# The output tail of an attention and spectral-mixing kernel: other items, and work moved to GpSimd and ScalarE

## The chip, the cores and the metric

The kernel runs on one core of one Trainium2 chip, with the other cores idle. The metric is the device time of one execution in microseconds. The engines are TensorE (PE in the profile, PEld for its weight loads), VectorE (DVE), ScalarE (ACT), GpSimd (POOL) and SyncE (SP), which here only issues DMAs.

## The reference

Attention with two kinds of masks for 8 batches of 576 rows, then a spectral layer. What the tail computes stands in the last lines:

```python
X = np.fft.rfft(x, axis=1)
Y = np.zeros_like(X)
Xr, Xi = (np.real(X[:, :n_modes]), np.imag(X[:, :n_modes]))
Yr = np.einsum('bmd,mde->bme', Xr, w_r) - np.einsum('bmd,mde->bme', Xi, w_i)
Yi = np.einsum('bmd,mde->bme', Xr, w_i) + np.einsum('bmd,mde->bme', Xi, w_r)
Y[:, :n_modes] = Yr + 1j * Yi
y = np.fft.irfft(Y, n=S, axis=1)
u = x + y
return (u + np.maximum(u @ w_ch, 0.0)).astype(np.float32)
```

Here x is the attention's output (8 batches, S = 576 rows, 512 columns), there are 64 modes, and w_r and w_i are 64 matrices of 512 x 512 each. The output is f32: 8 x 576 x 512 x 4 bytes = 9.44 MB.

## The kernel before

The kernel has three stretches. Attention runs first, with its two mask patterns one after the other. Beside its second half and after it the mode matrices stream in from HBM (cast to f16 on the way, issued from GpSimd's queue) and are multiplied with the spectra. The tail then turns spectra back into rows and writes the output.

The order of the instructions on each engine is the order of the program; no scheduler moves anything. Each engine takes its own instructions in order, and waits only where data or a buffer is missing. Pools hand out buffers in rotation: whoever asks for the next one waits until the last reader of what lay in it is done.

The tail splits the output into 18 items of two halves (128 rows x 512 columns each); 16 of them are four row groups t of two neighbouring batches, one half for each batch, and the last two hold the remaining 64 rows of four batches each. A row group with t = 0 or 1 holds the even or the odd rows of the first 256, t = 2 and 3 those of the next 256. By the time that the tail starts, the modes 0 to 47 are already in two kept parts, v0s (x and y times w_ch, f16) and xos (x plus y, f16); missing are the last 16 modes, whose spectra lie in zzs (times w_ch) and yys, four batches in one tile of 128 rows, 32 rows to a batch.

For item k there are two PSUM accumulators of two banks each:

- V: `v_early(k)` copies v0s in by two matmuls with the identity (line 1010), `new_rows(k, ..., zzs)` adds the last modes by two matmuls of 32 rows (line 1031). `v_done(k)` takes the relu on ScalarE into a buffer rl (line 1054).
- U: `u_early(k)` copies xos in the same way (line 1020), `new_rows(k, ..., yys)` adds the last modes. `u_done(k)` adds U and rl on VectorE into a slot of osb (line 1068), and SyncE stores the slot (line 1071).

In `pooled` halves (three of them before) the identity matmul for x is left out of U; GpSimd adds x to the relu instead (line 1057), ahead of VectorE's add.

The loop goes over steps k: V of item k and U of item k - 1 are made in one step. Items 0 and 1 are finished ahead of the loop, and in step 7 the spectra zzs of batches 4 to 7 are made (`spec_z(3, 1, held)`, line 758, and a ScalarE copy by `act_copy`, line 255). PSUM has three double buffers "p" and one "u": V and every even U take "p", the odd U takes "u". The buffers rl come from two tags with two buffers each,

```python
rl = ptr.tile([128, 2, 576], FP, tag=("xT", "rl")[k // 2 % 2], bufs=2, name="rl")
```

so item k + 4 takes the buffer of item k. osb has ten slots.

Four matmuls of 32 rows run side by side when their rows lie in four different quarters of the 128 partitions (quarter b % 4 for batch b). A3 holds the inverse transform's matrix four times, once for each quarter.

Of the kernel before, what the change touches and what calls it, by code (L numbers as in the profile page):

```python
# [12 lines left out]
AluOp = mybir.AluOpType  # L13
# [3 lines left out]
S = 576  # L17
D = 64
DM = 512
# [37 lines left out]
def kernel(  # L57
# [10 lines left out]
    nc = tc.nc  # L68
# [9 lines left out]
    def psum_pools(**bufs):  # L78
        pctx.close()
        pss.clear()  # L80
        for n, c in bufs.items():
            pss[n] = pctx.enter_context(
                tc.tile_pool(name="ps_" + n, bufs=c, space=PSUM)
            )

    def psum(kind, half=False, pair=False):
        if pair:
            return pss[kind].tile([128, 2, 512], FP, tag=kind, name=kind)
        if half:
            return pss[kind].tile([128, 1024], F16, tag=kind, name=kind)  # L90
        return pss[kind].tile([128, 512], FP, tag=kind, name=kind)
# [150 lines left out]
    def normalise(val, den, n, pieces, dst):  # L242
        rec = pin.tile([128, 8], FP, tag="rec", bufs=4, name="rec")
        nc.vector.reciprocal(out=rec[0:n, 0:pieces], in_=den)  # L244
        nc.vector.tensor_tensor(  # L245
            out=dst,
            in0=val.rearrange("p h (q c) -> p h c q", c=4),
            in1=rec[0:n, 0:pieces]
            .to_broadcast((n, pieces, 64))
            .rearrange("p h (q c) -> p h c q", c=4),  # L250
            op=AluOp.mult,
        )

    def act_copy(out, in_):
        nc.scalar.activation(out=out, in_=in_, func=ACTF.Copy)  # L255
# [463 lines left out]
    def row_cols(b, t):  # L719
        if t < 4:  # L720
            return ds(288 * (t % 2) + 32 * (b % 2) + 128 * (t // 2), 128)
        return ds(S + 64 * (b % 2), 64)
# [32 lines left out]
    def spec_z(g, bq, zp):  # L755
        for e in range(4):
            lhs = YS["YT"][:, e, g, ds(8 * bq, 8), :].rearrange("p x m -> p (x m)")
            nc.tensor.matmul(
                zp, lhs, w_chs["n"][:, e, :], start=(e == 0), stop=(e == 3)
            )  # L760
# [35 lines left out]
    def str_front(b):  # L796
        return [
            lambda: str_v(b, 0), lambda: str_v(b, 1),
            lambda: str_v(b, 2), lambda: str_q(b, 0),
            lambda: str_back(b, 0),  # L800
            lambda: str_back(b, 1), lambda: str_q(b, 1),
            lambda: str_k(b, 0),
            lambda: str_k(b, 1), lambda: str_k(b, 2),
        ]
# [12 lines left out]
    first = str_front(0)  # L817
# [73 lines left out]
    zzs = [ptr.tile([128, DM], F16, name=f"zz{i}") for i in range(B)]  # L891
    yys = [ptr.tile([128, DM], F16, name=f"yy{i}") for i in range(B)]
# [22 lines left out]
    for b in range(B + 1):  # L915
        for t in range(5):
            if b > 0 and (t < 4 or b % 2 == 0):
                work.append(lambda b=b, t=t: premix(b - 1, t))
            if b < B and t < 4:
                half, cp = ((1, 0), (1, 1), (0, 0), (0, 1))[t]  # L920
# [3 lines left out]
    A3 = cs["cFl"].rearrange("p a t m -> p (a t m)")[:, 0 : S + 128]  # L924
# [65 lines left out]
    for n, i in enumerate([3, 5, 7] + list(range(8, 21))):  # L990
        b, t = n // 2, n % 2 * 2
# [1 line left out]
        if n % 4 == 3:  # L993
            late.setdefault(i + (b == B - 1), []).append(lambda b=b: renew(b, (4,)))

    items = []
    for P0 in (0, 2):
        items += [((2 * P, 2 * P + 1), t) for t in range(4) for P in (P0, P0 + 1)]
    items += [(range(b, b + 4), 4) for b in (0, 4)]
    LAST = len(items) - 1  # L1000
    vps, ups, rls, osbs = {}, {}, {}, []

    def own(item, kept, half):
        bs, t = item
        return [kept[b][:, t] for b in bs] if t < 4 else [half[b // 2] for b in bs[::2]]

    def v_early(k):
        vps[k] = psum("p", pair=True)
        for j, r in enumerate(own(items[k], v0s, v0h)):
            nc.tensor.matmul(vps[k][:, j], idn, r, start=True, stop=False)  # L1010

    def pooled(k, j):
        return j == 1 and k in (4, 5, 6)

    def u_early(k):
        ups[k] = psum(("p", "u")[k % 2], pair=True)
        for j, r in enumerate(own(items[k], xos, xoh)):
            if pooled(k, j):
                continue
            nc.tensor.matmul(ups[k][:, j], idn, r, start=True, stop=False)  # L1020

    def new_rows(k, acc, spectra):
        bs, t = items[k]
        for j, b in enumerate(bs):
            q = ds(32 * (b % 4), 32)
            i = j // 2 if t == 4 else j
            o, cols = acc[:, i], row_cols(b, t)
            if t == 4:
                o = acc[ds(64 * (b % 2), 64), i]
            fresh = spectra is yys and pooled(k, i)  # L1030
            nc.tensor.matmul(  # L1031
                o, A3[q, cols], spectra[b // 4][q], start=fresh, stop=True
            )

    def out_rows(b, t):
        if t < 4:
            steps = [[2 * DM, 128], [(S + 64) * DM, 2], [1, DM]]
            first = 256 * (t // 2) + t % 2
        else:
            steps = [[DM, 128], [2 * S * DM, 2], [1, DM]]  # L1040
            first = 512
        return bass.AP(
            tensor=out.tensor, offset=out.offset + (S * b + first) * DM, ap=steps
        )

    def pieces(k):
        return [slice(0, 1), slice(1, 2)] if k in (0, 4, 5, 6) else [slice(0, 2)]

    def v_done(k):
        rl = ptr.tile([128, 2, 576], FP, tag=("xT", "rl")[k // 2 % 2], bufs=2, name="rl")  # L1050
        rls[k] = rl[:, :, 0:DM]
        vp = vps.pop(k)
        for j in [slice(0, 2)] if k else pieces(k):
            nc.scalar.activation(out=rls[k][:, j], in_=vp[:, j], func=ACTF.Relu)  # L1054
        for j, r in enumerate(own(items[k], xos, xoh)):
            if pooled(k, j):
                nc.gpsimd.tensor_tensor(
                    out=rls[k][:, j], in0=rls[k][:, j], in1=r, op=AluOp.add
                )

    def u_done(k):
        bs, t = items[k]
        up, rl = ups.pop(k), rls.pop(k)
        if not osbs:
            osbs.append(pw.tile([128, 2 * NWBUF, 2, DM], FP, tag="w", bufs=1, name="osb"))
        osb = osbs[0][:, k % (2 * NWBUF)]
        for j in pieces(k):
            nc.vector.tensor_tensor(
                out=osb[:, j], in0=up[:, j], in1=rl[:, j], op=AluOp.add
            )  # L1070
            nc.sync.dma_start(out_rows(bs[0], t)[:, j], osb[:, j])

    flush()
    rest = [(0, m) for m in range(SPLIT1, NM)] + [(1, m) for m in range(SPLIT0, NM)]
# [17 lines left out]

    for k in range(2):
        new_rows(k, vps[k], zzs)
    for k in range(2):
        v_done(k)
    for k in range(2):
        if k:
            u_early(k)
        new_rows(k, ups[k], yys)  # L1100
        u_done(k)
    for k in range(2, LAST + 2):
        if k == 7:
            held = psum("p", pair=True)[:, 0]
            spec_z(3, 1, held)
            act_copy(zzs[1], held)
        if k <= LAST:
            v_early(k)
        if k > 2:
            u_early(k - 1)  # L1110
        if k <= LAST:
            new_rows(k, vps[k], zzs)
        if k > 2:
            new_rows(k - 1, ups[k - 1], yys)
        if k <= LAST:
            v_done(k)
        if k > 2:
            u_done(k - 1)
    psum_pools()


# [28 lines left out]
```

## Time and profile before

| | |
|---|---|
| Three runs | 425.07, 425.74, 426.03 us (median 425.74) |
| Profiled execution, span from the first to the last instruction | 423.3 us |
| Share of the span: PE, DVE, ACT, POOL busy | 80%, 56%, 52%, 23% |
| DMA moved | 91.62 MB, mean 216 GB/s |
| SP's store queue, last 39 us | 9.44 MB |
| Median from issue to landing of a 512 KB store, of a 256 KB store | 3.4, 3.1 us |
| Mean granted TensorE clock | 0.942 |

Only the span is given of the profiled execution; the runs' times include what lies around the span. Busy shares are means over stretches with different limits, so the tail is read from its own windows.

### The profile page before, as it was taken

Reading aid. Unit: us, or ns where it says so; the run is one execution under the profiler, and the core shown is the slowest. Engines: PE = TensorE matmul, PEld = TensorE weight load, DVE = VectorE, ACT = ScalarE, POOL = GpSimd, SP = SyncE. Lnnn points to the kernel's source line nnn. Section 1 sums busy time; section 2 is a strip of 40 time slices with the busy share of each in tenths; the row PEclk is TensorE's granted clock in tenths of the full one; section 3 lists DMA queues with packets and bytes.
Section 4 is the critical chain, followed back from the end, with each engine's and each line's share of the span. In section 5 each row is a group of like instructions: output and inputs, shape, how many; then the busy total and the mean of one; then the engine's idle time right before and its main releaser. Section 6 shows DMA issues by size and latency. Waiting matters only on the chain.

```text
span 423.3 us, 9718 instructions
## 1 busy us (share of the span) xinstructions
PE 336.8 (80%) x4164; PEld 204.2 (48%) x4164; DVE 234.9 (56%) x470; ACT 218.8 (52%) x391; POOL 95.3 (23%) x165
## 2 busy tenths in 40 slices
PE   2977878779999198889874959896778989888994
PEld 2866766654666055556542425453344534445331
DVE  3788878851455034545323325864385547555794
ACT  1687778642656056565753323622162356443772
POOL 7332333322422011102122102212101232210200
PEclk9999999957999689999998789999798999999999
DMA  8999999999999999999999999999999999998598
GB/s 147 213 213 213 214 211 214 210 212 211 214 213 213 215 213 216 213 215 214 212 215 212 213 213 214 214 213 214 213 213 210 210 212 216 212 214 163 198 379 316
DMA packets 30346, 91.62 MB, mean 216 GB/s; under 512 B 3872, under 2 KB 4640, under 8 KB 30304
## 3 DMA queue, kind: packets, MB, share of 16 engines
q0 software_dynamic: 24624, 81.28, 96.9%
q1 hardware_dynamic: 5248, 9.65, 6.2%
q8 instruction: 32, 0.52, 0.5%
q10 hardware_dynamic: 432, 0.08, 0.1%
q14 instruction: 10, 0.08, 0.0%
HBM read 162.83 MB, written 9.44 MB: 407 GB/s over the span
## 4 chain that ended last, share of the span: by engine, by line
PE 38%; DMA 36%; DVE 15%; ACT 5%; issue 3%; POOL 1%; DVEq 0%; POOLq 0%; ACTq 0%
DMA wring<-in_moe_w_i_dram 28%; PE y L601 9%; PE sc L739 5%; DMA ring<-in_q_dram 5%; DMA wring<-in_moe_w_r_dram 4%; DVE xb L245 3%; DVE yy L774 2%; ACT X L255 2%; DVE kz L287 2%; PE p L1010 2%; PE y L536 2%; PE tp L417 2%; PE sc L463 2%; PE sc L536 1%; PE p L1031 1%
## 5 line engine op out<-in xcount | busy, mean ns | idle before, releaser
L601 PE MATMUL y<-wring,X 128*32 128x512 f16 (+1 forms) x424 | 65.0, 418 | 25.8 <-DMA wring<-in_moe_w_i_dram 25.7
L190 POOL DMA_DIRECT2D wring<-in_moe_w_r_dram x39 | 23.5, 604 | 200.1 <-PE y L601 176.8
L601 PEld LDWEIGHTS <-X 128*32 128x32 f16 (+1 forms) x448 | 27.5, 139 | 43.4 <-DMA wring<-in_moe_w_i_dram 26.5
L749 DVE COPY xo<-tp 128x512 f16<-128x512 f16 x32 | 22.1, 692 | 36.9 <-PE tp L747 36.8
L748 ACT ACTIVATE v<-sc 128x512 f16<-128x512 f32 x32 | 19.1, 597 | 45.1 <-PE sc L739 45.1
L255 ACT ACTIVATE yr<-y 128x512 f16<-128x512 f32 x28 | 16.7, 597 | 43.2 <-PE y L601 43.0
L739 PE MATMUL sc<-w_cp,xT 128*128 128x512 f16 x128 | 36.1, 404 | 1.9 <-DVE xT L707 1.9
L245 DVE TENSOR_TENSOR xb<-av,rec 90x256 f16<-90x256 f32 (+2 forms) x80 | 36.0, 450 | 2.8
L493 ACT ACTIVATE PL<-sc 128x480 f16<-128x480 f32 (+1 forms) x48 | 26.9, 578 | 20.2 <-PE sc L479 19.9
L244 DVE RECIPROCAL rec<-av 90x4 f32<-90x4 f32 (+2 forms) x80 | 14.6, 183 | 37.8 <-PE av L508 28.3
L424 DVE COPY qT<-tp 128x576 f16<-128x576 f16 x16 | 11.9, 752 | 39.3 <-PE tp L417 39.3
L190 POOL DMA_DIRECT2D wring<-in_moe_w_i_dram x42 | 25.4, 605 | 9.8 <-DMA wring<-in_moe_w_i_dram 3.8
L984 DVE TENSOR_TENSOR xo<-p,xo 128x1024 f16<-128x1024 f32 x16 | 19.6, 1225 | 13.8 <-PE p L782 13.8
L382 ACT ACTIVATE PL<-sc 90x360 f16<-90x360 f32 (+1 forms) x48 | 22.7, 490 | 6.9 <-PE sc L375 6.4
L255 ACT ACTIVATE v<-p 128x1024 f16<-128x1024 f32 x16 | 16.4, 1023 | 17.1 <-PE p L782 17.1
L255 ACT ACTIVATE v<-tp 128x640 f16<-128x640 f16 (+1 forms) x24 | 19.0, 807 | 11.6 <-PE tp L451 8.8
L417 PE MATMUL tp<-cI_s,ring 64*64 64x64 f16 x864 | 22.8, 198 | 2.1 <-DVE qT L424 1.7
L463 PE MATMUL sc<-cMl_s,cI_s 128*128 128x480 f16 (+1 forms) x48 | 18.9, 393 | 5.2 <-ACT PL L493 3.6
L255 ACT ACTIVATE kz<-tp 64x360 f16<-64x360 f16 (+1 forms) x32 | 18.9, 592 | 6.2 <-PE tp L417 5.2
L280 PE MATMUL tp<-cI_s,ring 72*128 72x72 f16 x256 | 15.4, 207 | 8.4 <-DMA ring<-in_v_dram 6.9
L417 PEld LDWEIGHTS <-ring 64*64 64x64 f16 x864 | 18.0, 112 | 8.3 <-issue 4.2
L1054 ACT ACTIVATE rl<-p 128x1024 f32<-128x1024 f32 (+1 forms) x19 | 18.4, 979 | 4.9 <-PE p L1031 3.0
(146 smaller groups left out, 736.6 us busy)
## 6 DMA issues: line engine op xcount, KB each, us to landing
wring<-in_moe_w_r_dram POOLq DMA_DIRECT2D x17, 1024.0 KB, 13.5
wring<-in_moe_w_i_dram POOLq DMA_DIRECT2D x16, 1024.0 KB, 17.7
wring<-in_moe_w_i_dram POOLq DMA_DIRECT2D x24, 512.0 KB, 15.3
wring<-in_moe_w_r_dram POOLq DMA_DIRECT2D x22, 512.0 KB, 13.4
out_dram<-osb SPq DMA_DIRECT2D x14, 512.0 KB, 3.4
ring<-in_v_dram POOLq DMA_DIRECT2D x8, 288.0 KB, 13.3
ring<-in_q_dram POOLq DMA_DIRECT2D x8, 288.0 KB, 13.6
ring<-in_k_dram POOLq DMA_DIRECT2D x8, 288.0 KB, 13.1
```

The costliest lines, as they stand in the source:

```text
L190: nc.gpsimd.dma_start(dst, rows)
L245: nc.vector.tensor_tensor(out=dst, in0=val.rearrange("p h (q c) -> p h c q", c=4), in1=rec[0:n, 0:pieces] .to_broadcast((n, pieces, 64)) . ...
L255: nc.scalar.activation(out=out, in_=in_, func=ACTF.Copy)
L382: nc.scalar.activation(out=PS[0:n, ds(POFF[t], 4 * n)], in_=scp[0:n, 0 : 4 * n], func=ACTF.Exp, scale=SCALE,)
L417: nc.tensor.transpose(tp[ds(64 * hp, 64), ds(64 * i, 64)], qn[ds(64 * hp, 64), ds(64 * (9 * g + i), 64)], idn[ds(64 * hp, 64), ds(64 * hp, ...
L463: nc.tensor.matmul(scp[:, 0 : n * times].rearrange("p (h x) -> p h x", h=times), idn, mask_rows("cMl", n, times), start=True, stop=False,)
L493: nc.scalar.activation(out=dst, in_=src, func=ACTF.Exp, scale=SCALE)
L601: nc.tensor.matmul(yp[ds(a, 32), :], Xh[half][pr, c].rearrange("p b r (h m) -> p (b r h) m", h=2)[:, :, mm % 32], wt[pr, XC[c], :], start= ...
L739: nc.tensor.matmul(vp, xT[:, ch], w_chs["cp"][:, ch, :], start=(ch == 0), stop=(ch == 3),)
L748: nc.scalar.activation(out=v0, in_=vp, func=ACTF.Copy)
L749: nc.vector.tensor_copy(out=xo.rearrange("p (h q c) -> p h q c", h=2, c=4), in_=tp[:, 0:512].rearrange("p (h c q) -> p h q c", h=2, c=4),)
L984: nc.vector.tensor_tensor(out=xo, in0=up[:, 0:n], in1=xo, op=AluOp.add)
```

## The change

- The items are cut differently: an item is now one batch and 256 of its rows (t = 2u and 2u + 1), so that a partition's two halves are two neighbouring rows of the output and a store writes runs of 4 KB in place of 2 KB. The batches come in the order 0, 2, 1, 3, first with u = 0, then with u = 1; then the same for 4 to 7. The last two items stay as they were.
- Both halves of an item now have the same batch and so the same quarter of the spectra. `swapped` copies each spectra tile on VectorE into a second one with its 64-row halves exchanged; the second half of an item (from item 2 on) reads that copy, two quarters on.
- U of an item is now made two steps after its V (`LAG = 2`). Item 1's U, which stood ahead of the loop, is finished in step 3.
- `pooled` now holds for the second halves of items 2, 3, 4, 6, 7, 9, 10, 12, 13 and 15.
- `lent` items are 5, 8, 11 and 14: ScalarE copies the second half of U into osb, and GpSimd adds the relu to it there; VectorE adds the first half only.
- A store is split in halves for the first and the last item, not for items 4, 5 and 6.

The core of the diff:

```diff
-    items = []
-    for P0 in (0, 2):
-        items += [((2 * P, 2 * P + 1), t) for t in range(4) for P in (P0, P0 + 1)]
+    items = [(b, u) for B0 in (0, 4) for u in range(2) for b in (B0, B0 + 2, B0 + 1, B0 + 3)]
     items += [(range(b, b + 4), 4) for b in (0, 4)]
     LAST = len(items) - 1
+    LAG = 2
...
     def pooled(k, j):
-        return j == 1 and k in (4, 5, 6)
+        return j == 1 and 2 <= k < LAST - 1 and not lent(k)
+
+    def lent(k):
+        return k in (5, 8, 11, 14)
...
+    def swapped(spectra, bq):
+        for i in range(2):
+            nc.vector.tensor_copy(
+                out=spectra[2 + bq][ds(64 * i, 64)], in_=spectra[bq][ds(64 - 64 * i, 64)]
+            )
...
+            for j in range(2):
+                turn = 2 * j if k > 1 else 0
+                todo.append(
+                    (
+                        acc[:, j],
+                        spectra[bs // 4 + turn],
+                        bs,
+                        2 * u + j,
+                        (bs + turn) % 4,
+                        spectra is yys and pooled(k, j),
+                    )
+                )
+        for o, src, b, t, q, fresh in todo:
+            q = ds(32 * q, 32)
+            nc.tensor.matmul(o, A3[q, row_cols(b, t)], src[q], start=fresh, stop=True)
...
+        if u < 4:
+            first = S * b + 64 * (b % 2) + 256 * u + j.start
+            steps = [[2 * DM, 128], [DM, j.stop - j.start], [1, DM]]
...
         for j in pieces(k):
+            by_vector = slice(0, 1) if lent(k) else j
+            if lent(k):
+                act_copy(osb[:, 1], up[:, 1])
+                nc.gpsimd.tensor_tensor(
+                    out=osb[:, 1], in0=osb[:, 1], in1=rl[:, 1], op=AluOp.add
+                )
             nc.vector.tensor_tensor(
-                out=osb[:, j], in0=up[:, j], in1=rl[:, j], op=AluOp.add
-            )
-            nc.sync.dma_start(out_rows(bs[0], t)[:, j], osb[:, j])
+                out=osb[:, by_vector], in0=up[:, by_vector], in1=rl[:, by_vector], op=AluOp.add
+            )
+            nc.sync.dma_start(out_rows(k, j), osb[:, j])
...
+    swapped(zzs, 0)
     for k in range(2):
         v_done(k)
-    for k in range(2):
-        if k:
-            u_early(k)
-        new_rows(k, ups[k], yys)
-        u_done(k)
-    for k in range(2, LAST + 2):
+    new_rows(0, ups[0], yys)
+    u_done(0)
+    swapped(yys, 0)
+    u_early(1)
+    for k in range(2, LAST + LAG + 1):
         if k == 7:
             held = psum("p", pair=True)[:, 0]
             spec_z(3, 1, held)
             act_copy(zzs[1], held)
+            swapped(zzs, 1)
+            swapped(yys, 1)
         if k <= LAST:
             v_early(k)
-        if k > 2:
-            u_early(k - 1)
+        if k > LAG + 1:
+            u_early(k - LAG)
         if k <= LAST:
             new_rows(k, vps[k], zzs)
-        if k > 2:
-            new_rows(k - 1, ups[k - 1], yys)
+        if k > LAG:
+            new_rows(k - LAG, ups[k - LAG], yys)
         if k <= LAST:
             v_done(k)
-        if k > 2:
-            u_done(k - 1)
+        if k > LAG:
+            u_done(k - LAG)
```

More of the change, by code (lines that the diff above doesn't have):

```diff
@@ L994 @@
             late.setdefault(i + (b == B - 1), []).append(lambda b=b: renew(b, (4,)))
-    items = []
-    for P0 in (0, 2):
-        items += [((2 * P, 2 * P + 1), t) for t in range(4) for P in (P0, P0 + 1)]
+    items = [(b, u) for B0 in (0, 4) for u in range(2) for b in (B0, B0 + 2, B0 + 1, B0 + 3)]
     items += [(range(b, b + 4), 4) for b in (0, 4)]
     LAST = len(items) - 1
+    LAG = 2
     vps, ups, rls, osbs = {}, {}, {}, []
     def own(item, kept, half):
-        bs, t = item
-        return [kept[b][:, t] for b in bs] if t < 4 else [half[b // 2] for b in bs[::2]]
+        b, u = item
+        return [half[x // 2] for x in b[::2]] if u == 4 else [kept[b][:, 2 * u + j] for j in range(2)]
     def v_early(k):
@@ L1020, in u_early @@
             nc.tensor.matmul(ups[k][:, j], idn, r, start=True, stop=False)
-    def new_rows(k, acc, spectra):
[L1023 to L1032, printed above, removed]
-            )
@@ L1035, in out_rows @@
[L1035 to L1038, printed above, removed]
-        else:
[L1040 to L1044, printed above, removed]
+    def swapped(spectra, bq):
[3 more added lines that the diff above has]
+            )
@@ new lines, in new_rows @@
+    def new_rows(k, acc, spectra):
+        bs, u = items[k]
+        if u == 4:
+            todo = [
+                (acc[ds(64 * (b % 2), 64), j // 2], spectra[b // 4], b, 4, b % 4, False)
+                for j, b in enumerate(bs)
+            ]
+        else:
+            todo = []
+            for j in range(2):
[13 more added lines that the diff above has]
+            nc.tensor.matmul(o, A3[q, row_cols(b, t)], src[q], start=fresh, stop=True)
@@ L1046, in pieces, with out_rows @@
+    def out_rows(k, j):
+        b, u = items[k]
+        if u < 4:
+            first = S * b + 64 * (b % 2) + 256 * u + j.start
+            steps = [[2 * DM, 128], [DM, j.stop - j.start], [1, DM]]
+        else:
+            first = S * b[0] + 512 + 2 * S * j.start
+            steps = [[DM, 128], [2 * S * DM, j.stop - j.start], [1, DM]]
+        return bass.AP(tensor=out.tensor, offset=out.offset + first * DM, ap=steps)
     def pieces(k):
-        return [slice(0, 1), slice(1, 2)] if k in (0, 4, 5, 6) else [slice(0, 2)]
+        return [slice(0, 1), slice(1, 2)] if k in (0, LAST) else [slice(0, 2)]
@@ L1052, in v_done @@
         vp = vps.pop(k)
-        for j in [slice(0, 2)] if k else pieces(k):
+        for j in pieces(k):
             nc.scalar.activation(out=rls[k][:, j], in_=vp[:, j], func=ACTF.Relu)
@@ L1061, in u_done @@
     def u_done(k):
-        bs, t = items[k]
         up, rl = ups.pop(k), rls.pop(k)
```

## The prediction

> **What bounds the kernel now.** I read the 40 slices first, then the last stage in windows, then the DMA view, the groups by shape and the timeline of that stage; all times are microseconds from the span's start. Items are numbered 0 to 17, in the order in which they are worked.
>
> ```profile
> DMA  8999999999999999999999999999999999998598
> GB/s 147 213 213 213 214 211 214 210 212 211 214 213 213 215 213 216 213 215 214 212 215 212 213 213 214 214 213 214 213 213 210 210 212 216 212 214 163 198 379 316
> ```
>
> ```profile
> 390.00:395.00 5.00, 4.04 (x41) 2.06 (x40) 1.96 (x6) 1.98 (x4) 0.00 (x0) 1.00 0.00 1
> 395.00:400.00 5.00, 4.97 (x30) 1.57 (x28) 4.52 (x5) 4.25 (x5) 0.48 (x1) 1.00 0.71 259
> 400.00:405.00 5.00, 5.00 (x33) 1.54 (x31) 4.41 (x7) 4.07 (x5) 2.91 (x3) 1.00 1.03 383
> 405.00:410.00 5.00, 5.00 (x35) 1.55 (x32) 4.72 (x5) 3.94 (x4) 0.00 (x0) 1.00 1.01 378
> 410.00:415.00 5.00, 5.00 (x34) 1.65 (x34) 4.42 (x5) 3.88 (x5) 0.00 (x0) 1.00 1.02 381
> 415.00:420.00 5.00, 2.01 (x17) 0.45 (x15) 3.29 (x3) 1.39 (x2) 0.00 (x0) 1.00 1.02 378
> ```
>
> ```profile
> q1 hardware_dynamic: 4960, 9.44, 65.2%
> ...
> out_dram<-osb SPq DMA_DIRECT2D x14, 512.0 KB, 3.4
> ```
>
> In the windows the columns are the length, busy time of PE, PEld, DVE, ACT and POOL, granted clock, DMA share and GB/s. Up to about 388 the weight loads set the pace (DMA 9 in every slice); the change doesn't touch that. It works on the tail from 393 on: 9.44 MB of output. From 400 to 420 the DMA engines are full (share 1.01 to 1.03) at 378 to 383 GB/s, mean 380. PE is full too. So the tail has two limits that lie close together: 512 KB at 380 GB/s take 1.38, and PE's period for an item is 1.30 (its successive v matmuls start at 407.72, 409.02, 410.32). In half-microsecond windows data starts at 395.85 and ends at 421.55; 18 x 1.38 = 24.8 of these 25.7 are transfer, 0.9 is starvation before 399.5. The last VectorE add ends at 418.6, and the queue drains for 3 more. The end is set by the DMA.
>
> ```profile
> L1054 ACT ACTIVATE rl<-p 128x1024 f32<-128x1024 f32 x17 | 17.4, 1024 | 4.5 <-PE p L1031 2.5 <-PE u L1031 1.4 <-DVE osb L1068 0.3
> L1068 DVE TENSOR_TENSOR osb<-u,rl 128x1024 f32<-128x1024 f32 x8 | 9.8, 1224 | 0.8 <-PE u L1031 0.4
> L1068 DVE TENSOR_TENSOR osb<-p,rl 128x512 f32<-128x512 f32 x6 | 3.9, 686 | 1.1 <-ACT rl L1054 0.5 <-POOL rl L1057 0.4 <-PE p L1031 0.2
> L255 ACT ACTIVATE zz<-p 128x512 f16<-128x512 f32 x1 | 0.6, 597 | 0.0
> ```
>
> ```profile
> 393.61 3.11 ACT L1054 ACTIVATE rl<-p 128x512 f32<-128x512 f32 x4 [0.48 <-PE p L1031]
> ...
> 395.65 1.23 DVE L1068 TENSOR_TENSOR osb<-u,rl 128x1024 f32<-128x1024 f32 x1
> ...
> 398.35 3.27 ACT L1054 ACTIVATE rl<-p 128x1024 f32<-128x1024 f32 x3 [0.27 <-PE u L1031]
> ...
> 399.52 3.39 POOL L1057 TENSOR_TENSOR rl<-rl,xo 128x512 f32<-128x512 f32 x3 [17.98 <-ACT rl L1054]
> ```
>
> The prices: relu of an item 1.02 on ACT, the whole add 1.22 and the half add 0.68 on DVE, a half copy out of PSUM 0.60 on ACT, a half add on GpSimd 1.13 in a row (3.39 for three) and 1.15 alone. GpSimd is slower than the engine it relieves, and POOL starts 0.15 after the relu that it waits for (398.35 + 1.02 = 399.37, then 399.52).
>
> **Part 1, 4 KB runs.** What a 4 KB store costs is not in the trace. Two rows bracket it: a 2 KB store packet takes 2048 x 16 / 380 = 86 ns; a weight load reads 8 KB a packet and runs at a mean of 213.5 GB/s written, so 4096 x 16 / 213.5 = 307 ns. The straight line through both gives 160 ns for 4 KB, that is 8 x 160 = 1.28 for an item on 16 engines. Ends: 1.38 (no gain) and 8 x 307 / 2 = 1.23. I take 1.28, between the two rows. Fifteen items (1 to 15) win 0.10 each; item 0, which goes out in halves, and items 16 and 17, whose rows don't adjoin, stay at 1.38. The most that this can give is 15 x 0.10 = 1.5, on the path.
>
> The Trainium skill (DMA: Bandwidth & Descriptors, section "Why small descriptors are slow (HBM only)") names a fixed cost of about 3 cycles a packet beside one cycle per 32 bytes. By it two 2 KB packets are 134 cycles and one of 4 KB is 131, so an item would take 1.35 (an estimate), and the transfers would win 0.5 instead of 1.5.
>
> **Part 2, the lag of two and the swapped copies.** Eight copies of 64x512 f16 come to DVE. Nearest rows: the f16 SBUF-to-SBUF operation at 128x320 takes 244 ns, at 128x384 260, so 0.25 ns an element and 292 ns at 512. Two stand before the first add: the yy copies end at 393.75, plus 0.58 is 394.33 against a start at 394.24, so at most 0.1. The four in step 7 (1.17) stand between items 4 and 5, where part 4 is later anyway.
>
> The order costs more. Before, item 1 was finished ahead of the loop; its add ran from 395.65 to 396.88. Now its yy rows come in step 3, behind two v pairs, and the second of these needs the p buffer that the relu of item 1 gives back (about 395.75: two half relus and a whole one after 393.61). Then 0.43 for the pair, 0.10 to change to 32-row weights, and 0.60 for two matmuls in one row group (0.22 + 0.38): DVE starts item 1 at 396.9 and ends at 398.1, 1.2 late. Its data flows 0.9 later (first add end 394.95, first data 395.85), at 399.0, while item 0 is gone by 395.85 + 1.38 = 397.2. Items 2, 3 and 4 follow at 1.22 each, to 401.8, and keep the queue just fed until about 404.
>
> **Part 3, GpSimd adds x to ten halves.** This takes one identity matmul of 0.22 from each; before, three had it, so PE loses 7 x 0.22 = 1.5. PE's period falls to 1.08. None of this shows: the DMA hides it, and so does part 4.
>
> **Part 4, the lent items 5, 8, 11, 14.** DVE saves 4 x (1.22 - 0.68) = 2.2, hidden as well. In its place comes a chain over ACT and GpSimd. With the lag, the relu of item k+2 and GpSimd's x half of k+2 are issued before the copy and the add of item k, and both engines take their work in order. For item 5: relu 6 ends at about 401.5 (as that relu did before); it frees the buffer for v of item 7; v and u 0.86, row change and rows 0.5, so relu 7 starts at 402.95 and ends at 404.0; 0.15 later POOL adds x for item 7 (1.13), then adds item 5 (1.15): 406.4. SP waits there for item 5's store, and item 6, done at about 405.2, is queued behind it. Data of item 5 flows at 407.3; the DMA was dry from about 404.
>
> The second link decides. The relu buffers come round every four items, so relu 9 writes the buffer that GpSimd reads in its add of item 5, and waits for it. From one lent add to the next: 0.05 to ACT, relu 1.02, 0.15 to POOL, x halves of two items 2 x 1.13, lent add 1.15, together 4.63 for three items, where the DMA needs 3 x 1.28 = 3.84. So GpSimd's chain becomes the bound: lent 8 ends at 411.05, lent 11 at 415.65. The last turn runs over ACT: 0.05, relus 15 and 16 2 x 1.02, copy 0.60, 0.15, lent add 1.15, so lent 14 ends at 419.65. Its store flows 0.9 later, at 420.55, and with it 15, 16 and 17, all but ready: 2 x 1.28 + 2 x 1.38 = 5.3, end of data 425.9.
>
> The lent add has two f32 inputs; the row has an f32 and an f16 one. By operations it is 1.15, by bytes (6 KB a partition against 5) 1.38: four times 0.23 or 0.9 more at the upper end. I take 1.15, the same shape. For this form the Trainium skill (GPSIMD Engine Reference, section 3.1) has a measured 4497 ns at 2048 elements, a quarter of which is 1.12; by that the sum would be 0.1 less.
>
> **The sum.** End of data 425.9 against 421.55: +4.3. The profiled span of 423.3 becomes 427.6. The runs lie 1.8 to 2.7 above that span (425.07 to 426.03), their median 2.44; on it the same 4.3 gives 430.0. About 0.2%, 0.85, is what a measurement here can tell from no change.
>
> **The rivals.**
> - *Only item 5 is late, then the DMA paces.* If relu 9 has slack that I don't see (GpSimd reaching its lent add before the next item's x half, or shorter turns), the loss is the gap before item 5: 407.3 + 11 x 1.28 + 2 x 1.38 = 424.1, +2.6, 428.3. For it: nothing in the trace of before shows a relu waiting for GpSimd. Against: the reuse of four buffers and both queues' order are in the code.
> - *GpSimd is slower here.* Lent adds at 1.38, and a little on the x halves where DVE works beside them: +0.9 and up, about 431.2. Against: the three adds beside DVE's took 1149 to 1153 ns.
> - *Faster: the DMA paces throughout.* One mechanism: stores at 1.28 are the only limit, because the lent adds come out before the queue is dry. 395.85 + 0.9 + 3 x 1.38 + 15 x 1.28 = 420.1, -1.45, 424.3. It decides if the lent add of item 5 ends before 403.2 (the queue dry at 399.0 + 4 x 1.28 = 404.1, less 0.9) and a turn is under 3.84. For it: DMA share 1.02 now; against: the chain over relu 7.
> - *The start eats the gain.* As the last one, but with item 1's data at 399.0: 399.0 + 15 x 1.28 + 2 x 1.38 = 421.0, -0.55, 425.2, no change that could be told.
>
> **How the numbers follow.** Forecast 430.0: 0.56; only item 5 late: 0.20; GpSimd slower: 0.12; DMA paces throughout: 0.07; the start eats it: 0.05. So slower 0.88, same 0.05, faster 0.07. The range takes the forecast, the case at 428.3 with 0.7 for store prices and handovers below it, and the one at 431.2 with 0.6 above: 427.6 to 431.8. The store's price hardly moves the forecast, as only the last four stores are on its path (1.23 to 1.38: -0.1 to +0.2).
>
> **What would show it.** Right: ACT's relu idle with GpSimd as releaser three times (items 9, 12, 15); lent adds 4.6 apart at about 406, 411, 415.7; DMA share well under 1 between 404 and 420; the add of item 1 at about 397. Part 1 is right if full windows show 400 to 420 GB/s. Wrong: DMA share 1.0 from 400 on (then the DMA paces), GpSimd adds far from 1.15, a lent add of item 5 that ends before 404, or a PE clock under 1.00 in the tail, since PE now idles a quarter of each turn.

## The result, and the profile after

Four runs of the changed kernel gave 429.19 to 431.98, median 430.59 us, against 425.88 for the kernel before (425.07 to 426.39, four runs on the same chip). The ratio is 1.0118, with a 95% interval of 1.0097 to 1.0139. The kernel is slower, by 4.7 us or 1.2%; the prediction was 430.0.

The profiled execution has a span of 430.2, and its run of 431.98 is the slowest of the four. Its tail begins 2.7 later than in the profile of before: ScalarE's copy of the first zzs starts at 395.23 in place of 392.54. In a second profile of the same changed kernel it starts at 393.67, and the tail behind it is the same to 0.04. The stretch ahead of the tail therefore scatters from run to run, and everything below is counted from the start of that copy ("zz + ..."). From there to the end of the output's data the kernel before takes 28.96, the changed one 33.17 and, in the second profile, 33.13. These 4.2 are what the change does in the tail. The medians differ by 4.7 here and by 4.8 in the second group of runs; what the rest of about 0.5 is stays open, since the stretch ahead of the tail scatters by more than that (the zz copy starts between 391.96 and 395.39 in the profiles of this document).

The first two fences are of the changed kernel: the DMA view of the tail (40 slices from 392 to 431, then the store queue), and windows of 5 us with the same columns as before.

```profile
DMA  0000001930999994007999299992999999999300
GB/s 0 0 0 0 0 0 40 378 137 0 370 399 403 412 408 160 0 0 294 408 395 412 105 391 408 399 407 97 403 395 416 399 412 387 382 376 389 118 0 0
...
q1 hardware_dynamic: 3008, 9.44, 61.5%
...
out_dram<-osb SPq DMA_DIRECT2D x16, 512.0 KB, 3.3
```

```profile
403.00:408.00 5.00, 4.21 (x25) 1.33 (x22) 4.07 (x8) 4.00 (x5) 2.72 (x4) 1.00 0.82 326
408.00:413.00 5.00, 4.29 (x28) 1.32 (x28) 3.52 (x4) 3.35 (x4) 3.87 (x4) 1.00 0.64 256
413.00:418.00 5.00, 4.09 (x25) 1.21 (x24) 3.32 (x5) 3.35 (x4) 3.87 (x4) 1.00 0.87 345
418.00:423.00 5.00, 3.96 (x26) 1.21 (x24) 3.32 (x4) 3.41 (x5) 2.70 (x3) 1.00 0.86 341
```

Before, the row of nines had no hole after the start. Now there are four, and between them the stores run at 391 to 416 GB/s, faster than the 380 of before; the 376 to 389 near the end are of items 16 and 17, which keep the 2 KB runs. No engine is busy for a whole window, and yet the DMA share falls to 0.64: something makes the engines wait for each other. Counted: data starts at zz + 3.47 (before 3.26). Of the 29.7 to its end, 15 x 1.29 + 3 x 1.38 = 23.5 are transfer, 1.3 less than the 24.8 of before, and 6.2 are idle, against 0.9. So the start gives 0.2, the transfers -1.3 and the idle time 5.3, together 4.2.

Who waits for whom shows in the view of waits of that stretch (total, times, longest), and the ring itself in the timelines of POOL and ACT.

```profile
DVE osb L1092 <- ACT osb L255: 5.5, 4, 1.7
...
ACT rl L1073 <- POOL osb L1089: 3.7, 3, 1.3
```

```profile
406.61 1.16 POOL L1076 TENSOR_TENSOR rl<-rl,xo 128x512 f32<-128x512 f32 x1 [1.31 <-ACT rl L1073]
407.72 1.27 POOL L1089 TENSOR_TENSOR osb<-osb,rl 128x512 f32<-128x512 f32 x1
410.13 2.27 POOL L1076 TENSOR_TENSOR rl<-rl,xo 128x512 f32<-128x512 f32 x2 [1.13 <-ACT rl L1073]
412.36 1.27 POOL L1089 TENSOR_TENSOR osb<-osb,rl 128x512 f32<-128x512 f32 x1
414.76 2.27 POOL L1076 TENSOR_TENSOR rl<-rl,xo 128x512 f32<-128x512 f32 x2 [1.14 <-ACT rl L1073]
416.99 1.27 POOL L1089 TENSOR_TENSOR osb<-osb,rl 128x512 f32<-128x512 f32 x1
```

```profile
409.03 1.94 ACT L1073 ACTIVATE rl<-p 128x1024 f32<-128x1024 f32 x2 [1.09 <-POOL osb L1089]
410.85 0.60 ACT L255 ACTIVATE osb<-p 128x512 f32<-128x512 f32 x1
411.33 1.04 ACT L1073 ACTIVATE rl<-p 128x1024 f32<-128x1024 f32 x1
413.66 1.94 ACT L1073 ACTIVATE rl<-p 128x1024 f32<-128x1024 f32 x2 [1.29 <-POOL osb L1089]
```

Read them together. GpSimd adds item 5 from 407.72 to 408.99 (line 1089). At 409.03 ScalarE, which had been idle for 1.09 with that add as releaser, starts relu 9. At 410.13, when relu 9 is done, GpSimd adds x for items 9 and 10, and at 412.36 item 8. One turn is 412.36 - 407.72 = 4.64, the next 416.99 - 412.36 = 4.63, each for three items that the DMA moves in 3 x 1.29 = 3.87. That leaves the holes of 0.7 to 0.8 before items 8 and 11. The hole of 2.8 before item 5 ends with the first lent add, but only half of it goes when nothing is lent (next section).

### The profile page after: what moved, and what is told of

It reads as the page before. It is cut to its first block, busy times and chain, and to the rows that moved or that the text cites. A ratio compares the mean times of both kernels' runs of the same rounds, so it can differ in the third digit from the quotient of the medians.

```text
span 430.2 us, 9729 instructions
## 1 busy us (share of the span) xinstructions
PE 340.9 (79%) x4157; PEld 204.3 (47%) x4157; DVE 234.7 (55%) x476; ACT 220.1 (51%) x396; POOL 108.5 (25%) x176
## 4 chain that ended last, share of the span: by engine, by line
PE 34%; DMA 26%; DVE 8%; ACT 5%; issue 3%; POOL 3%; DVEq 0%; POOLq 0%; ACTq 0%
DMA wring<-in_moe_w_i_dram 26%; PE y L601 10%; PE sc L739 5%; DVE yy L774 2%; PE tp L417 2%; PE y L536 2%; PE sc L463 2%; PE p L782 2%; ACT X L255 2%; ACT PL L493 1%; POOL rl L1076 1%; PE sc L479 1%; ACT rl L1073 1%; PE tp L747 1%; DVE xb L245 1%
```

## The experiments

Each group of runs shared a chip with the kernel before, whose median there was 425.65 to 425.76. "Tail" is the stretch from the start of the zz copy to the end of the data, from each profile; before it is 28.96. "Holes" are the stretches after its first data in which the DMA's share lies under a half, read to 0.1; the kernel before has 0.6 and 0.2, both near its start.

| | median us | ratio to before, 95% | tail | holes |
|---|---|---|---|---|
| changed kernel, again | 430.52 | 1.0107 (1.0086 to 1.0128) | 33.13 | 1.7, 2.8, 0.7, 0.8 |
| nothing lent | 427.09 | 1.0034 (1.0021 to 1.0047) | 30.29 | 1.7, 1.4 |
| own relu buffer | 429.63 | 1.0094 (1.0072 to 1.0117) | 32.68 | 1.7, 2.8, 0.5, 0.4 |
| own buffer, half first | 428.36 | 1.0060 (1.0040 to 1.0079) | 32.34 | 1.7, 2.9, 0.6 |
| lent work first | 426.82 | 1.0029 (1.0015 to 1.0042) | 30.89 | 1.7, 1.3, 0.4, 0.2 |
| 4 KB runs alone | 427.38 | 1.0041 (1.0025 to 1.0057) | 30.78 | 0.4, 0.7, 0.9, 1.0, 0.3 |
| copies off VectorE | 426.71 | 1.0022 (1.0009 to 1.0035) | 30.31 | 0.4, 0.5, 0.8, 0.8, 0.2, 0.4 |
| the same, x on GpSimd | 427.84 | 1.0050 (1.0032 to 1.0069) | 31.54 | 0.5, 0.4, 0.8, 0.8, 0.9, 0.4, 0.4 |
| 4 KB runs late | 425.34 | 0.9991 (0.9978 to 1.0004) | 29.14 | 0.6, 0.2, 0.4, 0.1, 0.3 |
| item 1 early | 427.86 | 1.0047 (1.0029 to 1.0065) | 31.17 | 0.5, 2.1, 1.5 |

The gain or loss against the kernel before comes out up to 0.8 apart by medians and by tails (lent work first: 1.2 and 1.9; own buffer, half first: 2.6 and 3.4). A difference between two variants that is smaller than that is settled only where both agree.

The changed kernel once more, in the second group:

> The changed kernel unchanged, as the reference for the runs on this chip: 430.6 (429.9 to 431.2), lent adds 4.6 apart, DMA gaps of 1.4, 2.8, 0.7 and 0.7.

430.52, tail 33.13, with lent adds at 406.17, 410.81 and 415.44: 4.64 and 4.63 apart. The ring repeats to a hundredth.

**Nothing lent.** The lent set is emptied; VectorE adds items 5, 8, 11 and 14 whole, everything else stays.

```diff
-        return j == 1 and 2 <= k < LAST - 1 and not lent(k)
+        return j == 1 and 2 <= k < LAST - 1 and k not in (5, 8, 11, 14)
 
     def lent(k):
-        return k in (5, 8, 11, 14)
+        return False
```

> The lent items are undone (VectorE adds both halves of items 5, 8, 11, 14; the ten pooled halves, the 4 KB runs, the swapped copies and the lag of two stay). Theory (GpSimd's chain with relus waiting for lent adds sets the tail): the three gaps of the DMA that lent items cause go; what is left is the gap of about 1.4 before item 1 and one before item 5 (VectorE's copies in step 7); item 5's data about 1.4 earlier, no later gaps: 3.0 less than the changed kernel, about 427.6 (427.0 to 428.2). Rival (the lag and the copies are the loss, not the lent items): gains less than 1, so 429.6 or more.

427.09, 3.4 less than the changed kernel's 430.52, and the tail is 2.8 shorter (33.13 - 30.29). The two late holes are gone and the one before item 5 halves, as the theory said. The rival, that the lag and the copies are the loss, falls as the main cause; but 1.4 over the kernel before remain, with the holes before item 1 and item 5. In VectorE's timeline of this kernel the add of item 5 starts as soon as the swapped copies of step 7 end:

```profile
404.07 0.59 DVE L1026 COPY yy<-yy 64x512 f16<-64x512 f16 x2
404.69 1.23 DVE L1092 TENSOR_TENSOR osb<-u,rl 128x1024 f32<-128x1024 f32 x1
```

**Own relu buffer.** This takes away one of the two things that a turn needs, relu k+4's wait for the lent add of k, by giving the lent items' relus two of osb's ten slots.

```diff
-        rl = ptr.tile([128, 2, 576], FP, tag=("xT", "rl")[k // 2 % 2], bufs=2, name="rl")
-        rls[k] = rl[:, :, 0:DM]
+        if lent(k):
+            rls[k] = osbs[0][:, 8 + k % 2]
+        else:
+            rl = ptr.tile([128, 2, 576], FP, tag=("xT", "rl")[k // 2 % 2], bufs=2, name="rl")
+            rls[k] = rl[:, :, 0:DM]
...
-        osb = osbs[0][:, k % (2 * NWBUF)]
+        osb = osbs[0][:, k % 8]
```

> As the changed kernel, but the relu of a lent item lies in a buffer of its own (two of osb's ten slots, output uses eight), so that relus 9, 12 and 15 have no GpSimd add to wait for. Theory: lent add of item 5 ends as before, at about 409, but the turns after it fall from 4.63 to under 3.9 and the DMA has no gap after item 5: 1.6 less than the changed kernel, about 429.0 (428.5 to 429.6). Rival (GpSimd's sheer work, or the order on its queue, sets the turn): within 0.4 of the changed kernel, with turns still near 4.6.

429.63: only 0.9 less, just outside the range that the theory gave, and the holes of 0.7 to 0.8 shrink to 0.4 to 0.5. The waits of ScalarE for GpSimd are gone, but the turn is still 409.79 - 405.41 = 4.38. The timelines of POOL and DVE of this kernel show why:

```profile
405.41 1.28 POOL L1092 TENSOR_TENSOR osb<-osb 128x512 f32<-128x512 f32 x1
...
409.79 1.27 POOL L1092 TENSOR_TENSOR osb<-osb 128x512 f32<-128x512 f32 x1
```

```profile
406.48 1.22 DVE L1095 TENSOR_TENSOR osb<-u,rl 128x1024 f32<-128x1024 f32 x1
409.12 0.69 DVE L1095 TENSOR_TENSOR osb<-p,osb 128x512 f32<-128x512 f32 x1 [1.42 <-ACT osb L255]
```

VectorE's half add of item 8 waits 1.42 for ScalarE's copy of the other half of item 8. The two read and write different columns, but the copy stands first in the program, and the wait fits a dependence that is kept for the whole slot; the next experiment tests it. The copy is queued behind relu 10, so VectorE is late, the PSUM buffer of U is late, PE's next u waits for it (0.62 at 409.86), and with it the next relu. There is a second ring behind the first, which the prediction didn't see.

**Own buffer, half first.** The same with VectorE's half add ahead of the copy in the program; on each engine the order is unchanged.

```diff
             if lent(k):
-                act_copy(osb[:, 1], up[:, 1])
-                nc.gpsimd.tensor_tensor(
...
             nc.vector.tensor_tensor(
...
+            if lent(k):
+                act_copy(osb[:, 1], up[:, 1])
+                nc.gpsimd.tensor_tensor(
...
```

> The kernel with own relu buffers, and VectorE's half add of a lent item stands ahead of ScalarE's copy in the program (the order on each engine is the same). In its trace VectorE's half add started only when that copy ended, 1.4 late, though the halves are different ones, and U of item k+2 and so its next relu waited for the half add. Theory of a second loop (copy of k behind relu k+2, half add behind the copy, PSUM of U k behind the half add): turns fall from 4.38 to under 3.9, the two DMA gaps of together 0.95 after item 5 go: 428.7 (428.1 to 429.2). Rival (GpSimd's three adds and handovers are the limit, or the wait only turns round): unchanged, 429.4 or more.

428.36, inside the theory's range. VectorE's wait for the copy is gone; its half add of item 8 now waits only for PE:

```profile
406.92 0.69 DVE L1090 TENSOR_TENSOR osb<-p,osb 128x512 f32<-128x512 f32 x1 [0.32 <-PE p L1053]
```

Not all came as expected: the turns are 4.49, 3.86 and 3.45 (lent adds at 404.55, 409.04, 412.90, 416.35), so one hole of 0.6 is left, and the tails of the two kernels differ by only 0.3 where the medians differ by 1.3. The second ring is shown; its price stays open between those two numbers.

**Lent work first.** No work changes. In the step of a lent item its copy and add stand ahead of the newest item's relu and x half on ACT and POOL.

```diff
+        if k > LAG and lent(k - LAG):
+            u_done(k - LAG)
         if k <= LAST:
             v_done(k)
-        if k > LAG:
+        if k > LAG and not lent(k - LAG):
             u_done(k - LAG)
```

> As the changed kernel, but in each step of a lent item its copy and add are issued ahead of the relu and the x half of the newest item (order on ScalarE, GpSimd and VectorE; no work is added or taken away). Theory: lent add of item 5 ends 1.5 earlier, at about 407.5, relus 9, 12, 15 don't wait, and the DMA paces from item 5 on: 3.1 less than the changed kernel, about 427.5 (426.9 to 428.2). Rival (the sum of GpSimd's and ScalarE's work is the limit): less than 1 gained, 429.6 or more.

426.82, 3.7 less than the changed kernel and just under the range that the theory gave; by the tails it is 2.2 less (33.13 - 30.89). The timeline of POOL of this kernel, to be read against the one of the changed kernel:

```profile
404.21 1.28 POOL L1089 TENSOR_TENSOR osb<-osb,rl 128x512 f32<-128x512 f32 x1 [0.92 <-ACT osb L255]
405.45 1.16 POOL L1076 TENSOR_TENSOR rl<-rl,xo 128x512 f32<-128x512 f32 x1
407.42 1.16 POOL L1076 TENSOR_TENSOR rl<-rl,xo 128x512 f32<-128x512 f32 x1 [0.81 <-ACT rl L1073]
408.54 1.27 POOL L1089 TENSOR_TENSOR osb<-osb,rl 128x512 f32<-128x512 f32 x1
```

The lent add of item 5 starts at zz + 11.0 (404.21 - 393.21) in place of zz + 12.5 (407.72 - 395.23), and the turns are 4.33, 3.85 and 4.15 (the next adds at 412.39 and 416.54). The same operations on the same engines cost 2.2 to 3.7 less in another order, so it is not the amount of GpSimd's work that sets the time. The tail is still 0.6 longer than with nothing lent.

**4 KB runs alone.** A lag of one, batches in the order 0, 1, 2, 3, item 1 ahead of the loop, x on GpSimd in items 4, 5, 6 as before, nothing lent.

```diff
-    items = [(b, u) for B0 in (0, 4) for u in range(2) for b in (B0, B0 + 2, B0 + 1, B0 + 3)]
+    items = [(b, u) for B0 in (0, 4) for u in range(2) for b in range(B0, B0 + 4)]
-    LAG = 2
+    LAG = 1
...
+    u_early(1)
+    new_rows(1, ups[1], yys)
+    u_done(1)
     swapped(yys, 0)
-    u_early(1)
...
```

> The 4 KB runs alone: items of one batch with the swapped copies, but a lag of one (batches in the order 0, 1, 2, 3, item 1 finished ahead of the loop), x added by GpSimd for items 4, 5, 6 as before, nothing lent. Theory: stores at about 406 GB/s, one short gap at the start as before, then TensorE's 1.30 for an item paces with the DMA's 1.29; end of data 0.5 to 1.1 earlier than before: 424.7 to 425.4, so faster than the kernel before. Rival (the copies and the new item order cost as much as the runs gain): within 0.3 of before or slower.

A miss: 427.38, slower than before by 1.7, where a gain was expected. The stores do run at about 405 GB/s, but VectorE delivers late. Its timeline in this kernel:

```profile
402.08 1.23 DVE L1092 TENSOR_TENSOR osb<-p,rl 128x1024 f32<-128x1024 f32 x1 [1.02 <-POOL rl L1076]
403.22 1.22 DVE L1092 TENSOR_TENSOR osb<-u,rl 128x1024 f32<-128x1024 f32 x1
404.46 0.59 DVE L1026 COPY zz<-zz 64x512 f16<-64x512 f16 x2
405.09 0.59 DVE L1026 COPY yy<-yy 64x512 f16<-64x512 f16 x2
405.71 1.23 DVE L1092 TENSOR_TENSOR osb<-p,rl 128x1024 f32<-128x1024 f32 x1
```

Item 4 waits 1.02 for its x half on GpSimd (its add is no longer split), and the four copies take 1.2 between items 5 and 6. Each makes a hole of about 1. The kernel before has a wait for GpSimd too (0.42) and no hole for it. The two periods suggest why: its stores take 1.38 for an item that is made in 1.30, so a queue builds up that covers it. With stores of 1.29 there is no queue to draw on, and every stall of the producers is seen at the end. That is argued from the periods; the last experiment bears on it.

**Copies off VectorE, without and with x on GpSimd.** Both are built on the 4 KB runs alone. The early copies go to GpSimd, the late one of zzs to ScalarE straight from PSUM, and GpSimd adds no x in the first and adds it from item 8 on in the second.

```diff
...
-            nc.vector.tensor_copy(
+            nc.gpsimd.tensor_copy(
                 out=spectra[2 + bq][ds(64 * i, 64)], in_=spectra[bq][ds(64 - 64 * i, 64)]
             )
...
-            swapped(zzs, 1)
-            swapped(yys, 1)
+            for i in range(2):
+                act_copy(zzs[3][ds(64 * i, 64)], held[ds(64 - 64 * i, 64)])
...
```

> 4 KB runs with a lag of one, no half given to GpSimd and nothing lent; the swapped copies are taken off VectorE (the first ones and those of yys on GpSimd, those of the late zzs on ScalarE straight from PSUM). Theory (in the kernel with the runs alone it was VectorE's copies and the first wait for GpSimd's adds that made the DMA dry, 2.6 in three gaps): TensorE paces as before the change, at 1.30, the gaps in step 7 and before items 2 and 4 go, the last add ends where it did before and the last half store takes 0.7 in place of 1.4: end of data 0.8 to 1.5 earlier than before, 424.2 to 424.9. Rival (TensorE's full row of identity matmuls, 1.30 an item against 1.29 of DMA, makes the DMA dry in step 7 for the whole 0.87 of spec_z and it never catches up): 425.3 to 426.

> As the one before, but GpSimd adds x to the second halves of items 8 to 15 (TensorE saves 8 x 0.22 = 1.7). Theory (a GpSimd add delays the first item by about 1.0 once, and VectorE at 1.22 and the DMA at 1.29 then pace): at best 0.3 better than without, at worst 0.6 worse: 424.0 to 425.4. Rival (TensorE is the limit of the one before): 0.7 or more better than that.

Both miss: 426.71 and 427.84. In the first the holes are 0.2 to 0.8 each, at the start, for spec_z in step 7, for PE's wait for the p buffer that ScalarE's copies hold, and at the last two items. The stated rival (PE at 1.30 can't catch up) was nearer, though its number was too low as well. In the second GpSimd's adds bring VectorE's wait for POOL back (1.02 and 0.82), and the time rises by 1.1. The 1.7 of matmuls that PE was spared came to nothing.

**Item 1 early.** As "nothing lent", with item 1's U finished ahead of the loop (the same edit of the start as in the 4 KB runs alone).

> The changed kernel with nothing lent, and item 1's U finished ahead of the loop again (the lag of two stays from item 2 on). Theory A (the place of item 1's rows costs 1.2 of the path): 1.2 less than with nothing lent alone, 425.9. Theory B (the lag of two as such delays item 2 as well, so the gap only moves from before item 1 to before item 2): within 0.4 of 427.1.

427.86: theory A is out, and theory B fits only in part, as it allowed 0.4 around 427.1. The hole moves from before item 1 to before item 2 and is 2.1 there. VectorE's timeline, and a line of the view of waits, show where the excess comes from:

```profile
397.04 1.23 DVE L1092 TENSOR_TENSOR osb<-u,rl 128x1024 f32<-128x1024 f32 x1
398.29 1.56 DVE L1026 COPY yy<-yy 64x512 f16<-64x512 f16 x2
400.38 1.22 DVE L1092 TENSOR_TENSOR osb<-p,rl 128x1024 f32<-128x1024 f32 x1 [0.53 <-PE p L1053]
```

```profile
PE p L1053 <- DVE yy L1026: 0.6, 1, 0.6
```

The swapped copies of yys now stand behind item 1's add, and take 1.56 in place of 0.59 (the last section returns to that). PE's last matmul for item 2 reads them: it runs at 399.91, 0.8 later than right behind the matmul before it (398.88 + 0.22). Without these 0.8 the holes at the start would be 0.5 + 1.3, about as much as the 1.7 before item 1 with nothing lent. So it isn't the place of item 1's rows that costs the time; the lag of two is what remains, though no kernel was run that has this start without the late copy.

**4 KB runs late.** The kernel before, with 4 KB runs only in items 8 to 15, where its queue is long. Two of the swapped copies that this needs run on VectorE in step 7 and two on GpSimd ahead of the loop, and the last store goes out in halves.

```diff
-    for P0 in (0, 2):
-        items += [((2 * P, 2 * P + 1), t) for t in range(4) for P in (P0, P0 + 1)]
+    items += [((2 * P, 2 * P + 1), t) for t in range(4) for P in (0, 1)]
+    items += [(b, 2 * u) for u in range(2) for b in range(4, 8)]
...
```

> The kernel before, with 4 KB runs only in items 8 to 15 (batches 4 to 7), where its DMA queue is full; the swapped zzs by two VectorE copies in step 7, the swapped yys by GpSimd ahead of the loop, the last store in halves. Theory (runs pay where the queue has a backlog to hide the copies behind): 8 x 0.09 = 0.7 less than before, 424.6 to 425.3, no DMA gap after the start. Rival (production falls behind the faster stores, as in the kernels with runs throughout): gaps in the DMA after step 8 and no gain, 425.6 or more.

425.34 against 425.65, ratio 0.9991 with an interval from 0.9978 to 1.0004: not told from no change. Its tail is 29.14, not shorter than before. The faster stores use up the queue, and from step 8 on the DMA waits for its producers instead (0.4, 0.1, 0.3). No version that was run is shown to beat the kernel before.

## Why the prediction was right

**The sum.** Data was to end 4.3 later; it ends 4.2 later in the tail. The forecast of 430.0 stands against 430.59 and 430.52, and the likeliest case is the one that came. The rest of about 0.5 was not in the sum, and its cause is open.

**The first link, the lent add of item 5.** Predicted to end at 406.4 on the clock of before. Measured 408.99; less the 2.69 by which this tail begins later, 406.3. The DMA was dry before it, from 407.0 to 409.85. Right.

**The second link, relus that wait for GpSimd.** Predicted: three relus idle with GpSimd as releaser, turns of 4.63, lent adds 8 and 11 ending at 411.05 and 415.65. Measured: three (3.7 in all), turns of 4.64 and 4.63, ends at 410.94 and 415.57 on the same clock. That the turn is right to 0.01 is luck: two errors cancel, all but 0.05, and the two x halves make up for most of that (2.23 in the turn in place of 2.26). The lent add takes 1.27, not 1.15: a row with an f16 input was taken for an operation with two f32 ones, and the truth lies between the two bounds given (1.15 and 1.38). The handover from ScalarE to GpSimd takes 0.08, not 0.15. The Trainium skill (GPSIMD Engine Reference, section 3.1) gives 4497 ns for 2048 elements; a quarter of that, 1.12, is an estimate, and the measured 1.27 decides.

**The last turn.** Predicted to run over ScalarE and to free the last four stores at 420.55. Lent 14 ended at 422.08 (419.4 on that clock), so its store could flow at 422.9. The queue was then busy with items 11 to 13 until about 423.0. The last turn did not bind, by a hair: it was lent 11 and the transfers behind it that set the end. Both sums give the same.

**The late item 1.** Predicted: its add at 396.9, 1.2 late, a dry stretch of 1.8. Measured 399.78 - 2.69 = 397.1, dry for 1.7. The size is right; the reason was put too narrowly, since with item 1 early the hole moved to item 2. What the step calls "the order" of item 1 points to the lag behind it.

**4 KB runs.** Predicted 1.28 an item by the line between two rows; windows of half a microsecond from 402 to 407 run at 393 to 418 GB/s, mean 406, so 1.29. The estimate of 1.35 by the Trainium skill's fixed cost a packet (DMA: Bandwidth & Descriptors, "Why small descriptors are slow (HBM only)") is too high: here the longer runs give more than that rule. What was wrong is the remark that this gain of up to 1.5 lies "on the path". With the copies and the item order that it needs, and nothing lent, it made the kernel slower in two versions (427.38 and 426.71). PE's 1.30 and the stalls of the start and of step 7 lie directly under the DMA's 1.38 and take its place. It was costed as if no other limit were near.

**Parts costed at nothing.** What PE and VectorE save is hidden, as said. The x halves themselves are not free: two of them are 2.23 of each turn, as the sum has it. The four copies in step 7 are hidden in the changed kernel behind the lent add of item 5; once that is gone, a hole of 1.4 is left there, with item 5's add right behind them.

**The rivals.** "Only item 5 is late" fails, since three relus did wait; and the version built for it (own relu buffer) shows that it would have failed anyway, through the second ring over VectorE's half add. "GpSimd is slower" came half true (1.27). "The DMA paces throughout" and "the start eats the gain" fail at the hole before item 5.

## What to carry to other kernels

Work that is moved to an idle engine has to be followed through every buffer and queue that it holds: here four adds of 1.27 on an engine with plenty of idle time, with the copies that feed them, cost 2.8 by the tails and 3.4 by the medians, because a relu four items on needs the buffer that they read, and because they stand in the queue behind the newest item's work. The same work, issued first, cost 0.6 by the tails and nothing that the medians show. When a transfer is made faster, look at the next limit and at the queue that hides the producers' stalls: with 1.38 against 1.30 there is a queue, with 1.29 against 1.30 there is none. And a dependence that is kept for a whole buffer can tie two engines together that touch different halves of it; the order in the program decides which of them waits.

## What the runs showed of the hardware

VectorE's two f16 copies of 64x512 inside SBUF take 0.59 with GpSimd idle (both pairs of step 7 in the 4 KB runs alone). They take longer when a GpSimd add runs beside them: in the changed kernel 1.10 for the pair at 404.65, with GpSimd adding from 404.15 to 405.31, and 0.59 for the pair right after it; with item 1 early 1.56.

```profile
404.15 1.16 POOL L1076 TENSOR_TENSOR rl<-rl,xo 128x512 f32<-128x512 f32 x1 [0.98 <-ACT rl L1073]
404.65 1.10 DVE L1026 COPY zz<-zz 64x512 f16<-64x512 f16 x2 [0.19 <-ACT zz L255]
405.78 0.59 DVE L1026 COPY yy<-yy 64x512 f16<-64x512 f16 x2
```

The copies wait for the end of the add rather than run slower beside it: the pair ends 0.44 after the add here (405.75 against 405.31), 0.45 in the 4 KB runs late (403.68 against 403.23) and 0.45 in the second pair of item 1 early (405.18 against 404.73), although the add had 0.66, 0.29 and 0.57 left when the pair began. VectorE's adds with one input in PSUM show nothing of the sort, 1.21 to 1.23 with or without GpSimd beside them. The Trainium skill (SBUF — State Buffer, section "Who interferes with whom") states that VectorE and GpSimd share one pair of ports under an exclusive lock; these rows agree with it, though no run here takes the lock apart from other causes. On GpSimd itself a copy of that shape takes 0.65 (1.28 for two), and an add of 128x512 takes 1.27 with two f32 inputs against 1.16 with one f32 and one f16.
